# Windowed attention and a gated feed-forward on one core: products without a reader on TensorE, a shorter start on DVE and SP, and a weights' conversion with one operation written otherwise

## The chip, the cores and the metric

The kernel runs on one core of one Trainium2 chip. The time is device time in microseconds (us) of one execution; lower is better. The engines are TensorE (PE, with its weight loads as PEld), VectorE (DVE), ScalarE (ACT), GpSimd (POOL) and SyncE (SP), which here only issues transfers.

## The reference

Attention over 4 batches, 8 heads, 768 positions and 64 channels a head, with a window of 128 positions and 4 sink positions, then a feed-forward layer from 512 to 2048 and back to 512 over all 3072 positions. All inputs are float32, n_sink and window are 64-bit integers.

```python
scores = matmul(q, k.T) / sqrt(64)
keep = (pos_k < n_sink) | ((rel >= 0) & (rel < window))   # rel = pos_q - pos_k
a = softmax(where(keep, scores, -1e9))
x = matmul(a, v)                       # heads side by side: 3072 x 512
h = x @ w_in                           # 3072 x 2048
g = h * clip(h + 3, 0, 6) / 6
out = g @ w_out                        # 3072 x 512
```

## The kernel before

The attention is cut into 48 units: 4 batches, 3 blocks of 256 positions (u) and 4 pairs of heads (p). A unit's stages are named by letters: A loads K, Q and V from DRAM; B splits K and Q into a high and a low part; C makes the scores on TensorE (L292 or L297), adds the mask and takes the row's extreme on DVE (L299), the exponential on ACT (L321), sum and reciprocal on DVE (L323, L324) and the division (L307 on ACT, L309 on DVE); D turns the result on TensorE (L341) and copies it out (L35); E multiplies it with V (L399) and splits the result into xh and xl (L35, L415). The first eight units with u = 0 are "plain": they are kept in f32 and multiplied in f32, where the later ones work in fp32r on high and low parts.

After four units of a block its feed-forward follows: eight times 24 products with w_in (L437), the gate on ACT and DVE (L443, L444, L41, L446), and 24 products with w_out (L457). The steps of this part are drained between the stages of the attention by the order string in L530.

The weights arrive as 64-bit words (the float32 pairs of `load_part`, L143) and are converted on the chip, 32 pieces of 128x512 values: two passes on ACT (L150, magnitude; L154, count), two on DVE (L156 takes the sign into the upper half of the count's word, L158 joins the shifted magnitude with it), one on ACT for the high part (L35) and one on DVE for the low part (L161). A piece passes through the buffers `st` (3 of them) and `wt` (3). `WN` (L532) says how many pieces are asked for in each unit.

At the start POOL makes two ramps (`rel`, `col`) and the identity, ACT's queue loads n_sink and window (`raw`), DVE makes the masks out of them (L101 to L111), and POOL makes masks for the later units (m_t0, m_t1). DVE also makes a flag out of n_sink and window (L564 to L570) that chooses a general path at the end, which these inputs do not take. Each engine loads the flag into a register (L574).

The order on each engine is not the order of the code. A scheduler lists the instructions by what is ready and by the place in the code, and each engine then runs its list strictly in order, waiting at each entry for what it needs.

Of the kernel before, what the change touches and what calls it, by code (L numbers as in the profile page):

```python
# [9 lines left out]
F32 = mybir.dt.float32  # L10
F32R = mybir.dt.float32r
I32 = mybir.dt.int32
BF16 = mybir.dt.bfloat16
U16 = mybir.dt.uint16
U32 = mybir.dt.uint32
ALU = mybir.AluOpType
# [3 lines left out]
P = 128  # L20
SK = 16
WMAX = 128
SCALE = 0.125
BIG = 1.0e30


# [18 lines left out]
def attn_ffn_kernel(ctx: ExitStack, tc: tile.TileContext, qx, kx, vx, vfx, vsx, n_sink, window, w_in, w_out, out):  # L45
    nc = tc.nc
# [8 lines left out]
    const = ctx.enter_context(tc.tile_pool(name="const", bufs=1))  # L55
    fast = ExitStack()
    work = fast.enter_context(tc.tile_pool(name="work", bufs=2))
    ps = fast.enter_context(tc.tile_pool(name="ps", bufs=8, space=PSUM))
# [4 lines left out]
    relf = rel.rearrange("p a b -> p (a b)")  # L63
# [5 lines left out]
    ident_r = const.tile([P, P], F32R, name="ident_r")  # L69
    ident0 = work.tile([P, P], F32, tag="st", name="ident0", bufs=3)  # L70
    make_identity(nc, ident0)
# [3 lines left out]
    nc.vector.memset(three, 3.0)  # L75


    raw = const.tile([P, 2, 2], I32, name="raw")
    nc.scalar.dma_start(out=raw[:, 0, :], in_=n_sink.bitcast(I32).partition_broadcast(P))
    nc.scalar.dma_start(out=raw[:, 1, :], in_=window.bitcast(I32).partition_broadcast(P))  # L80
    rawf = const.tile([P, 2, 2], F32, name="rawf")
# [6 lines left out]
                                   op0=ALU.mult, op1=ALU.add)  # L88
# [3 lines left out]
    W2 = 2 * P + SK  # L92
    WP = 2 * P + 2 * SK
    m_t0 = work.tile([P, W2], BF16, name="m_t0", bufs=1)
    m_t1 = work.tile([P, W2], BF16, name="m_t1", bufs=1)
# [3 lines left out]
    own, prev, snk = relf[:, P:2 * P], relf[:, 2 * P:3 * P], colf[:, P:2 * P]  # L99
# [6 lines left out]
    def bias_from(dst, keep, engine=nc.vector):  # L106
        engine.tensor_scalar(out=dst, in0=keep, scalar1=-1.0, scalar2=BIG, op0=ALU.add, op1=ALU.mult)

# [4 lines left out]
    bias_from(m_01[:, P:2 * P], own)  # L113
    bias_from(m_t0[:, 0:P], prev, nc.gpsimd)
    bias_from(m_t0[:, P:2 * P], own, nc.gpsimd)
    bias_from(m_t0[:, 2 * P:W2], snk[:, 0:SK], nc.gpsimd)
    nc.gpsimd.tensor_copy(out=m_t1[:, 0:P], in_=m_t0[:, 0:P])
    nc.gpsimd.tensor_copy(out=m_t1[:, P:P + SK], in_=m_t0[:, 2 * P:W2])
    nc.gpsimd.tensor_copy(out=m_t1[:, P + SK:W2], in_=m_t0[:, P:2 * P])

# [11 lines left out]
    def load_part(hi, lo, src, rows, at):  # L132
# [4 lines left out]
        if not wide:  # L137
            st = like(work.tile([P, 512], F32, tag="st", name="st", bufs=3))
# [7 lines left out]
        ft = it.bitcast(F32)  # L146
        half = st.rearrange("p n w -> p (n w)").bitcast(U16).rearrange("p (n w) -> p n w", w=4)

# [6 lines left out]
                             bias=7.5 * 2.0 ** -18 - 0.5)  # L155
        nc.vector.tensor_scalar(out=half[:, :, 1], in0=half[:, :, 3], scalar1=0x8000, scalar2=None,  # L156
                                op0=ALU.bitwise_and)
        nc.vector.scalar_tensor_tensor(out=it, in0=it, scalar=3, in1=low,  # L158
# [17 lines left out]
    ssc = work.tile([P, 2, P], F32R, name="ssc", bufs=1)  # L176
    nc.gpsimd.memset(vs.bitcast(F32), 0.0)
    nc.gpsimd.memset(ssc.bitcast(F32), 0.0)

# [335 lines left out]
    def slot_C(s, h, t):  # L515
        if 0 <= s < NS:
            C_score(s, h, t)
            if t == 1:
                C_soft(s, h)

    def slot_E(s, h):
# [11 lines left out]

    for s in range(NS + 2):
        for step in ORDER.split():
            if step == "-":
# [25 lines left out]

    fl = const.tile([P, 4], F32, name="fl")
    nc.vector.tensor_scalar(out=fl[:, 0:1], in0=ns_f, scalar1=float(SK), scalar2=None, op0=ALU.is_gt)  # L564
# [164 lines left out]
```

## Time and profile before

| | us |
|---|---|
| three runs, median | 764.99 (764.61 to 767.12) |
| the profiled execution | 765.18 |
| its span, first to last instruction | 763.3 |
| PE busy | 728.7 (95%) |
| PEld busy | 648.1 (85%) |
| DVE busy | 505.8 (66%) |
| ACT busy | 458.1 (60%) |
| POOL busy | 4.0 (1%) |

The rows shown in the prediction are of five kinds. A row of the page names an engine and 40 slices of the span with their busy tenths. A row of the timeline has start and length in us, engine, line, operation, the tile written and the tiles read, the shape, and in brackets how long the engine was idle before it and what ended that. A row of the chain of waits has start, length and what the last-ending chain of work was doing. A row of groups has line, engine, operation, shape and count, then busy us and mean ns, then idle us before it. A row of stages has a stretch of the span and the busy time of each engine in it.

### The profile page before, as it was taken

Reading aid. Unit: us, or ns where it says so; the run is one execution under the profiler, and the core shown is the slowest. Engines: PE = TensorE matmul, PEld = TensorE weight load, DVE = VectorE, ACT = ScalarE, POOL = GpSimd, SP = SyncE. Lnnn points to the kernel's source line nnn. Section 1 sums busy time; section 2 is a strip of 40 time slices with the busy share of each in tenths; the row PEclk is TensorE's granted clock in tenths of the full one; section 3 lists DMA queues with packets and bytes.
Section 4 is the critical chain, followed back from the end, with each engine's and each line's share of the span. In section 5 each row is a group of like instructions: output and inputs, shape, how many; then the busy total and the mean of one; then the engine's idle time right before and its main releaser. Section 6 shows DMA issues by size and latency. Waiting matters only on the chain.

```text
span 763.3 us, 13907 instructions
## 1 busy us (share of the span) xinstructions
PE 728.7 (95%) x4832; PEld 648.1 (85%) x4832; DVE 505.8 (66%) x1434; ACT 458.1 (60%) x1115; POOL 4.0 (1%) x17
## 2 busy tenths in 40 slices
PE   4999888889999999999999999999999999999996
PEld 2677677679999999999889999899889989999895
DVE  4679999967677766765776776765676776542331
ACT  4788889776766755755666666755665665511211
POOL 2000000000000000000000000000000000000000
PEclk9999999999999999999999999999999999999998
DMA  5456878455454544532644545434554442000000
GB/s 187 121 165 217 238 212 237 138 142 132 128 134 122 134 125 105 140 95 67 166 110 114 143 107 127 120 82 102 146 130 116 128 114 72 15 15 1 28 1 32
DMA packets 57134, 89.87 MB, mean 118 GB/s; under 512 B 8672, under 2 KB 40416, under 8 KB 57056
## 3 DMA queue, kind: packets, MB, share of 16 engines
q1 hardware_dynamic: 56768, 88.90, 43.1%
q8 instruction: 40, 0.66, 0.4%
q14 instruction: 38, 0.31, 0.1%
q10 hardware_dynamic: 288, 0.00, 0.0%
HBM read 41.68 MB, written 6.29 MB: 63 GB/s over the span
## 4 chain that ended last, share of the span: by engine, by line
PE 78%; DVE 10%; ACT 5%; DMA 3%; issue 2%; SPq 1%; ACTq 0%; DVEq 0%
PE o L457 30%; PE hps L437 30%; PE av L399 7%; PE pt L341 4%; PE sp L297 4%; PE sp L292 2%; DMA K<-kt 1%; ACT Pt L307 1%; DVE st L156 1%; ACT Pt L321 1%; DVE wt L158 1%; DVE gf L444 1%; DVE Pt L299 1%; DMA raw<-in_window_dram 1%; DVE g L446 1%
## 5 line engine op out<-in xcount | busy, mean ns | idle before, releaser
L437 PE MATMUL hps<-xh,wih 128*128 128x256 f32 x768 | 219.9, 286 | 2.1 <-ACT wih L35 1.9
L437 PE MATMUL hps<-xh,wil 128*128 128x256 f32 x768 | 216.1, 282 | 1.6 <-DVE wil L161 1.6
L437 PE MATMUL hps<-xl,wih 128*128 128x256 f32 x768 | 215.5, 281 | 0.0
L457 PE MATMUL o<-woh,gh 128*128 128x512 f32 x384 | 156.2, 407 | 6.6 <-DVE gh L41 2.4
L457 PE MATMUL o<-woh,g 128*128 128x512 f32 x384 | 152.8, 399 | 1.9 <-DVE g L446 1.9
L457 PE MATMUL o<-wol,gh 128*128 128x512 f32 x384 | 152.5, 397 | 0.0
L437 PEld LDWEIGHTS hps<-xh,wih 128*128 128x128 f32 x768 | 145.7, 190 | 5.3 <-ACT wih L35 3.9
L437 PEld LDWEIGHTS hps<-xh,wil 128*128 128x128 f32 x768 | 145.2, 189 | 3.4 <-DVE wil L161 3.3
L437 PEld LDWEIGHTS hps<-xl,wih 128*128 128x128 f32 x768 | 145.6, 190 | 1.4
L321 ACT ACTIVATE Pt<-Pt,nb 128x272 f32<-128x272 f32 (+2 forms) x160 | 81.1, 507 | 73.3 <-DVE nb L299 71.3
L443 ACT ACTIVATE gf<-hps,three 128x512 f32<-128x512 f32 x96 | 65.9, 686 | 88.9 <-PE hps L437 88.4
L444 DVE SCALAR_TENSOR_TENSOR gf<-gf,hps 128x512 f32<-128x512 f32 x96 | 66.0, 687 | 67.0 <-ACT gf L443 65.8
L457 PEld LDWEIGHTS o<-woh,g 128*128 128x128 f32 x384 | 72.6, 189 | 21.8 <-DVE g L446 5.1
L457 PEld LDWEIGHTS o<-woh,gh 128*128 128x128 f32 x384 | 72.6, 189 | 19.1 <-DVE gh L41 3.1
L299 DVE CUSTOM_DVE_ANT_0 Pt<-sp,m_t 128x272 f32<-128x272 f32 x128 | 55.8, 439 | 49.5 <-PE sp L297 49.0
L307 ACT ACTIVATE Pt<-Pt,rc 128x272 f32<-128x272 f32 (+2 forms) x158 | 72.1, 502 | 25.9 <-DVE rc L324 24.7
L457 PEld LDWEIGHTS o<-wol,gh 128*128 128x128 f32 x384 | 72.6, 189 | 11.1 <-DVE wol L161 0.3
L446 DVE TENSOR_TENSOR g<-gf,gh 128x512 fp32r<-128x512 f32 x96 | 66.2, 690 | 1.1
L30 DVE TENSOR_TENSOR pl<-pt,ph 128x512 fp32r<-128x512 f32 (+1 forms) x80 | 52.8, 661 | 18.4 <-ACT ph L35 17.8
L297 PE MATMUL sp<-K,Q 128*128 128x272 f32 (+2 forms) x320 | 64.1, 288 | 0.7 <-DMA Q<-qt 0.4
L35 ACT ACTIVATE ph<-pt 128x512 fp32r<-128x512 f32 (+1 forms) x80 | 46.3, 578 | 29.5 <-PE pt L341 28.2
L297 PEld LDWEIGHTS sp<-K,Q 128*128 128x128 f32 x320 | 53.2, 189 | 8.1 <-DVE gf L444 0.7
(91 smaller groups left out, 944.0 us busy)
## 6 DMA issues: line engine op xcount, KB each, us to landing
K<-kt SPq DMA_DIRECT2D x128, 200.0 KB, 3.5
Q<-qt SPq DMA_DIRECT2D x160, 64.0 KB, 2.4
st<-in_w_in_dram SPq DMA_DIRECT2D x16, 512.0 KB, 4.7
st<-in_w_out_dram SPq DMA_DIRECT2D x16, 512.0 KB, 5.0
kr<-in_kx_dram SPq DMA_DIRECT2D x32, 200.0 KB, 2.6
qr<-in_qx_dram SPq DMA_DIRECT2D x48, 128.0 KB, 2.2
vr<-in_vx_dram SPq DMA_DIRECT2D x32, 192.0 KB, 2.6
out_dram<-ost SPq DMA_DIRECT2D x24, 256.0 KB, 2.3
```

The lines of the kernel that those rows point to most:

```text
L30: lo_engine.tensor_tensor(out=lo, in0=src, in1=hi.bitcast(F32), op=ALU.subtract)
L35: nc.scalar.mul(out=out, in_=src, mul=scale)
L297: nc.tensor.matmul(out=sp[:, 0:w], lhsT=Q[:, h, t * P:(t + 1) * P], rhs=K[:, h, part, k0c:k0c + w], start=(part == 0), stop=(part == 1))
L299: nc.vector.tensor_tensor_reduce(out=cell(s, h, t, 0, w), in0=sp[:, 0:w], in1=m[:, 0:w], scale=-SCALE, scalar=3.0e38, op0=ALU.add, op1=ALU ...
L307: nc.scalar.mul(out=blk, in_=blk, mul=c)
L321: nc.scalar.activation(out=blk, in_=blk, func=AF.Exp, scale=-1.0, bias=nb[:, i:i + 1], accum_out=sm[:, i:i + 1])
L399: nc.tensor.matmul(out=o, lhsT=l, rhs=r, start=(j == 0 and (h == 0 or not plain(s))), stop=(j == len(seq) - 1 and (h == 1 or not plain(s))))
L437: nc.tensor.matmul(out=hp[:, half, :], lhsT=l, rhs=r, start=(j == 0), stop=(j == n - 1))
L443: nc.scalar.activation(out=gf, in_=hp, func=AF.Relu, bias=three, scale=1.0)
L444: nc.vector.scalar_tensor_tensor(out=gf, in0=gf, scalar=6.0, in1=hp, op0=ALU.min, op1=ALU.mult)
L446: eng(GLO, state["n"] * NP).tensor_tensor(out=g, in0=gf, in1=gh.bitcast(F32), op=ALU.subtract)
L457: nc.tensor.matmul(out=acc, lhsT=l[:, f, ts_], rhs=r[i][:, f, :], start=(i == 0 and f == 0 and j == 0), stop=(i == NFP - 1 and f == 1 and ...
```

## The change

Two batches of ten products without a reader are put on TensorE (`keep_busy`): one ahead of the first scores, one behind the exponentials of the second head of unit 0. They multiply the ramp `rel` with itself in f32 and write a PSUM tile that nothing reads. The load of window goes from ACT's queue to SP's. The identity's scratch takes the buffer `kt` instead of one of the three `st`. The flag's scratch takes one of the three rotating buffers `nb`, so its operations can only follow the last units that use them. The later masks and two clearings are written into a function that is called at the head of unit 3. L156 and its 16-bit view give way to one operation on 32-bit words that masks the sign and joins it with the count.

```diff
+WARM = (10, 10)
...
-    ident0 = work.tile([P, P], F32, tag="st", name="ident0", bufs=3)
+    ident0 = work.tile([P, P], F32, tag="kt", name="ident0", bufs=1)
...
+    def keep_busy(n):
+
+        idle = ps.tile([P, 512], F32, tag="bank", name="idle")
+        for _ in range(n):
+            nc.tensor.matmul(out=idle[:, 0:P], lhsT=relf[:, 0:P], rhs=relf[:, 0:P], start=True, stop=True)
+
+    keep_busy(WARM[0])
...
-    nc.scalar.dma_start(out=raw[:, 1, :], in_=window.bitcast(I32).partition_broadcast(P))
+    nc.sync.dma_start(out=raw[:, 1, :], in_=window.bitcast(I32).partition_broadcast(P))
...
-    bias_from(m_t0[:, 0:P], prev, nc.gpsimd)
-    bias_from(m_t0[:, P:2 * P], own, nc.gpsimd)
-    bias_from(m_t0[:, 2 * P:W2], snk[:, 0:SK], nc.gpsimd)
-    nc.gpsimd.tensor_copy(out=m_t1[:, 0:P], in_=m_t0[:, 0:P])
-    nc.gpsimd.tensor_copy(out=m_t1[:, P:P + SK], in_=m_t0[:, 2 * P:W2])
-    nc.gpsimd.tensor_copy(out=m_t1[:, P + SK:W2], in_=m_t0[:, P:2 * P])
...
-        nc.vector.tensor_scalar(out=half[:, :, 1], in0=half[:, :, 3], scalar1=0x8000, scalar2=None,
-                                op0=ALU.bitwise_and)
+        nc.vector.scalar_tensor_tensor(out=low, in0=high, scalar=-2 ** 31, in1=low,
+                                       op0=ALU.bitwise_and, op1=ALU.bitwise_or)
...
-    nc.gpsimd.memset(vs.bitcast(F32), 0.0)
-    nc.gpsimd.memset(ssc.bitcast(F32), 0.0)
+
+    def later_constants():
+
+        bias_from(m_t0[:, 0:P], prev, nc.gpsimd)
...
+        nc.gpsimd.memset(vs.bitcast(F32), 0.0)
+        nc.gpsimd.memset(ssc.bitcast(F32), 0.0)
...
             if t == 1:
                 C_soft(s, h)
+                if s == 0 and h == 1:
+                    keep_busy(WARM[1])
...
     for s in range(NS + 2):
+        if s == 3:
+            later_constants()
...
-    fl = const.tile([P, 4], F32, name="fl")
+    fl = work.tile([P, 4], F32, tag="nb", name="fl", bufs=3)
```

The order on TensorE at the start of the program, before (sp are scores, pt the turned probabilities):

```order
L292 MATMUL sp<-kr,qr 128x128
L292 MATMUL sp<-kr,qr 128x256
L292 MATMUL sp<-kr,qr 128x128
L292 MATMUL sp<-kr,qr 128x256
L341 MATMUL pt<-ident_r,Ph 128x128 x4
```

and now (the line numbers of the changed kernel are up to 14 higher, so L302 is L292 and L351 is L341):

```order
L81 MATMUL idle<-rel 128x128 x10
L302 MATMUL sp<-kr,qr 128x128
L302 MATMUL sp<-kr,qr 128x256
L302 MATMUL sp<-kr,qr 128x128
L302 MATMUL sp<-kr,qr 128x256
L81 MATMUL idle<-rel 128x128 x10
L351 MATMUL pt<-ident_r,Ph 128x128 x4
```

The two batches stand ahead of the first scores and between them and the first transpositions; nothing else moves there.

The order on ACT at the start, before (Ph is the f32 score tile, st and wt are buffers of the weights' conversion):

```order
L79 DMA raw<-in_n_sink_dram 128x2
L80 DMA raw<-in_window_dram 128x2
L321 ACT_TABLE_LOAD
L321 ACTIVATE Ph,sm<-Ph,nb 128x128
L321 ACTIVATE Ph,sm<-Ph,nb 128x256
L321 ACTIVATE Ph,sm<-Ph,nb 128x128
L321 ACTIVATE Ph,sm<-Ph,nb 128x256
L307 ACTIVATE Ph<-Ph,rc 128x256
L150 ACTIVATE wt<-st 128x512
```

and now (L151 is L150, L155 is L154, L331 is L321):

```order
L87 DMA raw<-in_n_sink_dram 128x2
L151 ACT_TABLE_LOAD
L151 ACTIVATE wt<-st 128x512
L155 ACTIVATE st<-st 128x512
L151 ACTIVATE wt<-st 128x512
L155 ACTIVATE st<-st 128x512
L151 ACTIVATE wt<-st 128x512
L35 ACTIVATE wih_111<-wt 128x512
L155 ACTIVATE st<-st 128x512
L331 ACTIVATE Ph,sm<-Ph,nb 128x128
L331 ACTIVATE Ph,sm<-Ph,nb 128x256
```

Seven operations of the weights' conversion now stand ahead of the first exponential.

The order on DVE behind the first two heads' score tiles, before:

```order
L299 ISA Ph,nb<-sp,m_90 128x256
L299 ISA nb 128x1
L323 TENSOR_SCALAR sm<-sm 128x2
L324 RECIPROCAL rc<-sm 128x2
L309 TENSOR_SCALAR Ph<-Ph,rc 128x128
```

and now (L309 is L299, L162 is L161, L159 is L158, L157 stands in the place of L156, L333, L334 and L319 are L323, L324 and L309):

```order
L309 ISA Ph,nb<-sp,m_101 128x256
L309 ISA nb 128x1
L162 TENSOR_TENSOR wil_119<-wt,wih_111 128x512
L333 TENSOR_SCALAR sm<-sm 128x2
L159 SCALAR_TENSOR_TENSOR wt<-wt,st 128x512
L334 RECIPROCAL rc<-sm 128x2
L333 TENSOR_SCALAR sm<-sm 128x2
L157 SCALAR_TENSOR_TENSOR st<-st 128x512
L319 TENSOR_SCALAR Ph<-Ph,rc 128x128
```

Three operations of the weights' conversion now stand between the last score tile and the first division.

More of the change, by code (lines that the diff above doesn't have):

```diff
@@ L13 @@
 BF16 = mybir.dt.bfloat16
-U16 = mybir.dt.uint16
 U32 = mybir.dt.uint32
@@ L146, in load_part @@
         ft = it.bitcast(F32)
-        half = st.rearrange("p n w -> p (n w)").bitcast(U16).rearrange("p (n w) -> p n w", w=4)
         nc.scalar.activation(out=ft, in_=high.bitcast(F32), func=AF.Abs, scale=2.0 ** -112)
@@ L176, in attn_ffn_kernel @@
     ssc = work.tile([P, 2, P], F32R, name="ssc", bufs=1)
-    nc.gpsimd.memset(vs.bitcast(F32), 0.0)
-    nc.gpsimd.memset(ssc.bitcast(F32), 0.0)
+    def later_constants():
+        bias_from(m_t0[:, 0:P], prev, nc.gpsimd)
+        bias_from(m_t0[:, P:2 * P], own, nc.gpsimd)
+        bias_from(m_t0[:, 2 * P:W2], snk[:, 0:SK], nc.gpsimd)
+        nc.gpsimd.tensor_copy(out=m_t1[:, 0:P], in_=m_t0[:, 0:P])
+        nc.gpsimd.tensor_copy(out=m_t1[:, P:P + SK], in_=m_t0[:, 2 * P:W2])
+        nc.gpsimd.tensor_copy(out=m_t1[:, P + SK:W2], in_=m_t0[:, P:2 * P])
+        nc.gpsimd.memset(vs.bitcast(F32), 0.0)
+        nc.gpsimd.memset(ssc.bitcast(F32), 0.0)
     def batch_loads(b):
```

## The prediction

> **What bounds the kernel now.** I read the clock row of the page first, then TensorE's rows in order of time, then the chain of waits, then busy time by stage. The page's clock row says full speed from the first slice on:
>
> ```profile
> PEclk9999999999999999999999999999999999999998
> ```
>
> TensorE's own rows say otherwise. In the first block of the feed-forward part (L437) equal 128x256 products start 0.22 us apart, and a microsecond later 0.12 us apart:
>
> ```profile
> 48.19 0.41 PE L437 MATMUL hps<-xh,wil 128*128 128x256 f32 x1
> 48.41 0.41 PE L437 MATMUL hps<-xh,wih 128*128 128x256 f32 x1
> ...
> 49.57 0.28 PE L437 MATMUL hps<-xh,wih 128*128 128x256 f32 x1
> 49.69 0.28 PE L437 MATMUL hps<-xl,wih 128*128 128x256 f32 x1
> ```
>
> So until 49.3 us TensorE works at half its later pace, and the row does not show it. The chain of waits says the same: one set of f32 scores (L292) or of f32 products with V (L399) takes 1.58 us there, and 0.85 us later on.
>
> ```profile
> 22.69 1.58 PE sp L292 x4
> ...
> 26.17 1.58 PE sp L292 x4
> 27.74 1.58 PE av L399 x4
> ```
>
> ```profile
> 59.68 0.85 PE sp L292 x4
> 60.53 0.85 PE av L399 x4
> ```
>
> By stage (columns: length, then busy us and instructions of PE, PEld, DVE, ACT, POOL, then granted clock, DMA share, GB/s):
>
> ```profile
> 12.00:50.00 38.00, 36.04 (x107) 24.38 (x108) 23.17 (x82) 28.53 (x74) 0.00 (x0) 1.00 0.49 156
> ...
> 80.00:100.00 20.00, 15.31 (x84) 12.56 (x83) 18.32 (x49) 17.16 (x43) 0.00 (x0) 0.91 0.85 244
> ...
> 120.00:140.00 20.00, 17.69 (x114) 14.66 (x112) 18.94 (x44) 17.44 (x39) 0.00 (x0) 1.00 0.76 238
> 140.00:180.00 40.00, 35.70 (x240) 31.59 (x241) 30.16 (x84) 26.15 (x65) 0.00 (x0) 0.96 0.46 124
> 180.00:300.00 120.00, 119.81 (x860) 110.76 (x859) 85.05 (x246) 79.13 (x194) 0.00 (x0) 1.00 0.50 127
> ```
>
> Three stages: from 12 to 50 us a slow TensorE (95% busy), then to about 150 us DVE with ACT close behind (the weights' conversion: 92 to 95%), then TensorE at full pace. The last stage does the same work in both kernels, so what the change wins or loses before 160 us comes out one for one at the end.
>
> **The change part by part.** *Start of ACT.* In the kernel before, the weights' loads stand on SP behind the branch flag, and ACT takes its first exponentials first (the start of the row is in us, then how long it took):
>
> ```profile
> 6.86 0.15 DVE L564 TENSOR_SCALAR fl<-nw 128x1 f32<-128x1 f32 x1
> ...
> 7.56 0.28 DVE L101 TENSOR_SCALAR rel<-rel,nw 128x128 f32<-128x128 f32 x1
> ...
> 9.15 0.80 SPq L143 DMA_DIRECT2D st<-in_w_in_dram  x2
> ...
> 9.50 0.28 DVE L299 CUSTOM_DVE_ANT_0 Ph<-sp,m 128x128 f32<-128x128 f32 x1
> ...
> 9.82 0.40 ACT L321 ACTIVATE Ph<-Ph,nb 128x128 f32<-128x128 f32 x1 [6.86 <-DVE nb L299]
> ...
> 11.98 1.36 PE L341 MATMUL pt<-ident_r,Ph 128*128 128x128 f32 x4 [4.60 <-DVE Ph L309]
> ...
> 12.97 0.66 ACT L150 ACTIVATE wt<-st 128x512 f32<-128x512 f32 x1 [0.58 <-DMA st<-in_w_in_dram]
> ```
>
> Taking the flag's six operations away brings the masks forward by 7.56 - 6.86 = 0.70 us, and that is worth nothing by itself: in the new order of ACT the first exponential stands behind seven operations of the conversion, three L150, three L154 and one L35, which need the weights.
>
> ```profile
> L154 ACT ACTIVATE st<-st 128x512 int32<-128x512 uint32 x32 | 21.3, 665 | 0.0
> L150 ACT ACTIVATE wt<-st 128x512 f32<-128x512 f32 x32 | 21.3, 665 | 2.4 <-DMA st<-in_w_out_dram 1.8 <-DMA st<-in_w_in_dram 0.6
> ...
> L35 ACT ACTIVATE wih<-wt 128x512 fp32r<-128x512 f32 x16 | 10.0, 625 | 2.2 <-DVE wt L158 2.1
> ```
>
> They take 3 x 0.665 + 3 x 0.665 + 0.625 = 4.6 us. The first weights landed 12.97 - 9.15 = 3.8 us after their issue. They now go out behind seven issues of 0.4 us and a little (0.80 for the two in the row above), at about 4 us, but also behind 1 MB of K, Q and V; I take 8.5 us for the landing (bounds: 4 + 3.8 = 7.8, and 9.8 if the transfers before them delay them by 2 us). The first exponential then starts at 8.5 + 4.6 = 13.1 us instead of 9.82: 3.3 us later. Behind the exponentials DVE now does one L161, one L158 and one operation in the place of L156 ahead of the first L309, which the first transposition waits for:
>
> ```profile
> L156 DVE TENSOR_SCALAR st<-st 128x512 uint16<-128x512 uint16 x32 | 24.0, 750 | 3.4 <-ACT st L154 3.1
> L158 DVE SCALAR_TENSOR_TENSOR wt<-wt,st 128x512 int32<-128x512 int32 x32 | 22.0, 689 | 0.5
> ...
> L161 DVE TENSOR_TENSOR wil<-wt,wih 128x512 fp32r<-128x512 f32 x16 | 11.0, 687 | 1.1 <-ACT wih L35 1.1
> ```
>
> That is about 2.1 us, of which I take 1.0 to lie under the exponentials: 1.1 us more. The first transposition so moves from 11.98 to about 16.4 us: **+4.4 us** (bounds +3.7 and +5.7), and the slow TensorE behind it, 95% busy, carries this to 50 us.
>
> *What is bought with it.* The first and the fifth L444 frame the stage in which DVE bounds the kernel:
>
> ```profile
> 51.60 0.69 DVE L444 SCALAR_TENSOR_TENSOR gf<-gf,hps 128x512 f32<-128x512 f32 x1 [0.39 <-ACT gf L443]
> ...
> 81.65 0.68 DVE L444 SCALAR_TENSOR_TENSOR gf<-gf,hps 128x512 f32<-128x512 f32 x1
> ```
>
> By the first DVE has done, counting its rows in order, 10 sign steps, 9 L158 and 8 L161 instead of 7, 7 and 6: 3 x 0.75 + 2 x 0.69 + 2 x 0.69 = 5.0 us of DVE's work ahead of it that stood behind it. By the fifth the counts are level again (19, 18, 18 against 19, 19, 19). Between the two DVE bounds the kernel, so the lead is worth **-5.0 us** there (bounds: 0 if something else bounds that stage, -6.4 if all three conversions are whole).
>
> *Sign and count joined.* 32 L156 of 0.75 us become 32 operations like L158, on three strided operands instead of two. Where the next operation needs the result, DVE went on after 0.78 us, where it does not, after 0.53 us:
>
> ```profile
> 76.51 0.74 DVE L156 TENSOR_SCALAR st<-st 128x512 uint16<-128x512 uint16 x1
> 77.04 0.45 DVE L299 CUSTOM_DVE_ANT_0 Ph<-sp,m 128x256 f32<-128x256 f32 x1
> ...
> 85.69 0.75 DVE L156 TENSOR_SCALAR st<-st 128x512 uint16<-128x512 uint16 x1 [0.22 <-ACT st L154]
> 86.47 0.69 DVE L158 SCALAR_TENSOR_TENSOR wt<-wt,st 128x512 int32<-128x512 int32 x1
> ```
>
> With 0.69 us the joined one saves 0.06 in the first case and may lose some 0.07 in the second. With some 24 of the first and 8 of the second: 1.4 - 0.5 = **-0.9 us** (bounds -1.9, all of the first kind, and +1.0, if the third strided operand costs 0.06 more).
>
> *Products without a reader.* Each is a 128x128 product in f32, two instructions. From the 1.58 us of four instructions over 768 columns, one of 128 takes about 0.26 to 0.29 us at the slow pace, so ten take 5.2 to 5.8 us. The first ten need only the IOTA of L65, which ends at 0.84 + 0.24 = 1.1 us, and end at about 6.9. The first scores could begin at 5.72 before:
>
> ```profile
> 0.84 0.24 POOL L65 IOTA rel<- 128x128 f32 x1 [0.39 <-POOLq L712]
> ...
> 5.72 1.66 PE L292 MATMUL sp<-kr,qr 64*128 64x128 f32 x8 [5.72 <-DMA qr<-in_qx_dram]
> ```
>
> The 1.2 us are covered: the scores end by 8.6 us, DVE reaches them after 9 us. Were that cover gone, they would cost 1.2 us. The second ten end at about 14.4 us, before the first transposition at 16.4; with a first exponential at 9.82, as now, they would have cost 2.4 us. **0**, unless they change TensorE's pace. I say they do not, for long enough: from 22.69 to 29.32 us TensorE does f32 products without a pause, 6.6 us, more than half of them on all 128 rows, and stays slow; the fp32r products of one block of L437 brought the faster pace (first rows above). And a pace gained is lost in idle time:
>
> ```profile
> 80.32 0.81 PE L399 MATMUL av<-pf,VF 128*128 128x256 f32 x4
> 83.28 0.53 PE L457 MATMUL o<-woh,gh 128*128 128x512 f32 x1 [2.14 <-DVE sm L323]
> ```
>
> After these 2.14 idle us the granted clock falls (0.91 over that stage, above), and the changed kernel idles 2 us or more ahead of its first transposition.
>
> The Trainium skill (TensorE: Matmul & The Clock Gate, Part 1, the HAM clock gate) puts it as time: "Whatever you issue in your first ~3.4 µs runs at 1.2 GHz; everything after runs at 2.4 GHz." By that the first batch alone would bring the fast pace. The trace agrees for fp32r, and disagrees for the f32 stretch of 6.6 us.
>
> *The rest.* The identity in another buffer frees the third weights' buffer at once (in the loads above). The window's load ahead of K on SP puts the scores some 0.45 us later, covered by the masks. The later masks and the two clearings stand on POOL in the same order as before; POOL works 4.0 us in all, so that edit is 0. The flag's operations now stand late on DVE, before the last stage, and SP reads the flag with six output transfers behind it: 1.0 us of DVE under a TensorE that is 99.8% busy: 0.
>
> **Sum.** +4.4 - 5.0 - 0.9 = -1.5 us. The profiled execution took 765.18 us (span 763.3 and 1.9 around it) and lies 0.2 us above the median of 764.99. 765.18 - 1.5 - 0.2 = **763.5 us**; its own range, with the bounds above, is 760 to 767.
>
> **Rivals.** *TensorE gets fast early and stays so.* This is the skill's rule worked out here. For it: the batches run on full 128 rows for some 13 us, a stretch that the trace before does not have (its scores use 64 rows). Against it: the 6.6 us, and that the f32 stretches alone would have to hold the pace. The head would then be bound by ACT: 28.53 us busy in 12 to 50 us, plus 2.5 conversions of about 1.95 us more: 33 us from 16.4, so the first L444 at about 50 instead of 51.6. That is -1.5, with the lead and the sign -1.5 - 5.0 - 0.9 = -7.4: 757.6 us.
>
> *The delay stays and the lead is lost.* In the middle stage DVE also waits for transfers:
>
> ```profile
> 132.95 6.03 DMA K<-kt
> 139.03 3.96 DMA vr<-in_vx_dram
> ```
>
> If earlier weights only move the waits of SP's queue (K, Q and V stand in it behind the weights' loads, which wait for a free buffer), the 5.0 us of DVE's work turn into idle time at this place. Against it: DVE is 92 to 95% busy there, so there is little idle time to turn them into. 4.4 - 0.9 = +3.5: 768.5 us. It decides from the point where these 10 us end no earlier than now.
>
> *The change does not do what it says:* the conversions, though first in order, do not come earlier because their loads land late; then the delay is small too, and only the sign counts: 764.1 us.
>
> **Chances.** Forecast 0.45, early fast TensorE 0.33, lost lead 0.17, only the sign 0.05. A measurement of this kernel tells 0.3%, 2.3 us, from no change: below 762.7 is faster, above 767.3 slower. Of the forecast's 0.45 some 0.18 lie below 762.7, 0.02 above 767.3. Faster 0.33 + 0.18 = 0.51; slower 0.17 + 0.02 and a rest of 0.01 = 0.20; same 0.29. The range runs from 756.5, which holds most of the second case, to 767.5, which leaves out most of the third.
>
> **What would show it.** In the changed profile: a first exponential near 13 us and a first transposition near 16.4 (late loads: later still); scores and products with V of 1.58 us up to the first L437, against 0.85 if the batches work; the first L444 near 56 us, and the fifth, at 81.65 before, at about 80.5 (74 with a fast TensorE, 85 with a lost lead); the joined operation near 0.69 us. The forecast is wrong if the pace changes before 45 us, or if ACT does not wait for weights at the start.

## The result, and the profile after

The changed kernel takes **776.73 us** (median of 4, 774.42 to 777.48) against 765.43 us (median of 4, 764.61 to 767.12) of the kernel before, run beside it: a ratio of 1.0138, 95% interval 1.0117 to 1.0159. It is slower by some 11 us, outside the predicted range. Its profiled execution took 774.42 us, 9.2 us more than that of before, and is the fastest of the four; the traces below account for these 9.2 us.

The head of the changed kernel, TensorE in order of time (these lines stand ten lines lower in the changed kernel: L302 is L292, L351 is L341, L409 is L399, L447 is L437, L467 is L457, L454 is L444; L81 are the products without a reader):

```profile
1.13 4.21 PE L81 MATMUL idle<-rel 128*128 128x128 f32 x20 [1.13 <-POOL rel L65]
5.76 0.93 PE L302 MATMUL sp<-kr,qr 64*128 64x128 f32 x8 [0.42 <-DMA qr<-in_qx_dram]
6.62 2.50 PE L81 MATMUL idle<-rel 128*128 128x128 f32 x20
16.60 1.24 PE L351 MATMUL pt<-ident_r,Ph 128*128 128x128 f32 x4 [7.48 <-DVE rc L334]
...
20.26 1.65 PE L409 MATMUL av<-pf,VF 128*128 128x256 f32 x4
```

The products do bring the fast pace: the eight instructions of the first scores take 0.93 us instead of 1.66. Then TensorE idles 7.48 us for the first transposition and the pace is gone: the products with V take 1.65 us for four, as before. The clock row of the page shows the half pace now, in its first three slices of 19.3 us, which it did not in the kernel before:

```profile
PEclk7569989999999999999999999999999999999999
```

ACT behind that idle time (its first conversion, L151, and behind the seven operations of the conversion its first exponential, L331):

```profile
9.43 0.66 ACT L151 ACTIVATE wt<-st 128x512 f32<-128x512 f32 x1 [6.96 <-DMA st<-in_w_in_dram]
...
13.61 0.40 ACT L331 ACTIVATE Ph<-Ph,nb 128x128 f32<-128x128 f32 x1
```

The joined sign operation takes what was predicted (mean 688 ns):

```profile
L157 DVE SCALAR_TENSOR_TENSOR st<-st 128x512 int32<-128x512 int32 x32 | 21.9, 688 | 3.6 <-ACT st L155 3.5
```

The stages behind the head, cut at the same gates (the first L444, the one at 81.65 us, which is the fourth in the trace and not the fifth as the prediction counts, and the one at 145.43 us). Before (length, busy us of PE, PEld, DVE, ACT, POOL, granted clock, DMA share, GB/s):

```profile
51.60:81.65 30.05, 29.28 (x168) 23.06 (x166) 28.17 (x77) 27.14 (x64) 0.00 (x0) 1.00 0.65 195
81.65:145.43 63.78, 55.55 (x346) 46.63 (x347) 59.53 (x143) 54.37 (x121) 0.00 (x0) 0.97 0.78 227
```

After:

```profile
57.10:82.84 25.74, 25.17 (x143) 19.75 (x142) 22.50 (x60) 21.58 (x53) 0.00 (x0) 1.00 0.59 188
82.84:152.76 69.92, 60.09 (x358) 50.81 (x358) 61.29 (x153) 55.65 (x126) 0.00 (x0) 0.93 0.70 207
```

The first of the two stages is 4.3 us shorter: the lead of the conversions is real, and the changed kernel is only 1.2 us behind at 82.84 us. The second is 6.1 us longer. DVE's idle time in it is 8.6 us (69.92 - 61.29) against 4.3 us before; the other 1.8 us are DVE's own work, 61.29 us against 59.53. TensorE idles 9.8 us against 8.2, and its granted clock is 0.93 against 0.97: as an estimate from these two figures, 4.9 us of full speed are missing (0.07 x 69.92) instead of 1.9 (0.03 x 63.78). The largest single place, TensorE first:

```profile
99.46 0.73 PE L467 MATMUL o<-woh,gh 128*128 128x512 f32 x2 [1.79 <-ACT woh L35]
...
101.52 0.63 PE L467 MATMUL o<-woh,g 128*128 128x512 f32 x1
...
105.81 0.39 PE L467 MATMUL o<-woh,g 128*128 128x512 f32 x1
110.86 0.58 PE L447 MATMUL hps<-xh,wih 128*128 128x256 f32 x1 [4.66 <-ACT wih L35]
```

and ACT at the same time:

```profile
102.69 0.52 ACT L317 ACTIVATE Pt<-Pt,rc 128x272 f32<-128x272 f32 x1 [1.99 <-DVE rc L334]
...
106.01 0.69 ACT L453 ACTIVATE gf<-hps,three 128x512 f32<-128x512 f32 x1 [2.37 <-PE hps L447]
...
106.90 0.66 ACT L151 ACTIVATE wt<-st 128x512 f32<-128x512 f32 x1
...
110.17 0.63 ACT L35 ACTIVATE wih<-wt 128x512 fp32r<-128x512 f32 x1 [0.93 <-DVE wt L159]
```

TensorE idles 1.79 us, its next products take 0.63 us instead of 0.39, ACT stands 2.37 us ahead of a gate that these products make late, the next conversion (L151) is queued behind that gate, and TensorE then idles 4.66 us for this very conversion. Before, the largest wait of TensorE in this stage was 2.14 us. A second place follows at 122.72 us, where TensorE waits for the sink positions' V (`raw_s`, split into `vs`); before, no wait for it in this stage reaches 0.2 us. Behind it the products of L467 are slow again (0.63 us):

```profile
122.72 0.39 PE L409 MATMUL av<-pz,vs 128*128 128x256 f32 x1 [1.91 <-DVE vs L30]
...
125.00 0.63 PE L467 MATMUL o<-woh,g 128*128 128x512 f32 x1
```

From about 180 us on the two kernels run nearly in parallel, but not quite: 7.1 us apart at 315 us, 9.2 at the last outputs.

### The profile page after: what moved, and what is told of

It reads as the page before. It is cut to its first block, busy times and chain, and to the rows that moved or that the text cites. A ratio compares the mean times of both kernels' runs of the same rounds, so it can differ in the third digit from the quotient of the medians.

```text
span 772.7 us, 13996 instructions
## 1 busy us (share of the span) xinstructions
PE 737.9 (96%) x4872; PEld 659.7 (85%) x4872; DVE 505.5 (65%) x1434; ACT 456.8 (59%) x1115; POOL 3.9 (1%) x17
## 4 chain that ended last, share of the span: by engine, by line
PE 76%; DVE 7%; ACT 7%; DMA 5%; issue 2%; SPq 1%; ACTq 0%; DVEq 0%
PE o L467 30%; PE hps L447 29%; PE av L409 6%; PE sp L307 4%; PE pt L351 4%; DMA st<-in_w_in_dram 2%; PE sp L302 2%; ACT Pt L317 1%; ACT Pt L331 1%; DMA st<-in_w_out_dram 1%; ACT wt L151 1%; DVE wt L159 1%; DMA raw_s<-in_vsx_dram 1%; DMA Q<-qt 1%; DVE gf L454 1%
## 5 line engine op out<-in xcount | busy, mean ns | idle before, releaser
L447 PE MATMUL hps<-xh,wih 128*128 128x256 f32 x768 | 222.0, 289 | 6.1 <-ACT wih L35 5.7
L447 PE MATMUL hps<-xh,wil 128*128 128x256 f32 x768 | 217.5, 283 | 0.0
L447 PE MATMUL hps<-xl,wih 128*128 128x256 f32 x768 | 216.6, 282 | 0.0
L467 PE MATMUL o<-woh,gh 128*128 128x512 f32 x384 | 156.7, 408 | 5.6 <-DVE gh L41 3.8
L447 PEld LDWEIGHTS hps<-xh,wih 128*128 128x128 f32 x768 | 145.4, 189 | 10.2 <-ACT wih L35 7.9
L467 PE MATMUL o<-woh,g 128*128 128x512 f32 x384 | 153.6, 401 | 0.4 <-DVE g L456 0.4
L467 PE MATMUL o<-wol,gh 128*128 128x512 f32 x384 | 152.9, 399 | 0.0
L447 PEld LDWEIGHTS hps<-xl,wih 128*128 128x128 f32 x768 | 145.5, 189 | 1.3
L447 PEld LDWEIGHTS hps<-xh,wil 128*128 128x128 f32 x768 | 145.0, 189 | 0.9 <-DVE wil L162 0.5
L331 ACT ACTIVATE Pt<-Pt,nb 128x272 f32<-128x272 f32 (+2 forms) x160 | 81.2, 507 | 77.5 <-DVE nb L309 75.9
L453 ACT ACTIVATE gf<-hps,three 128x512 f32<-128x512 f32 x96 | 66.0, 687 | 91.6 <-PE hps L447 90.9
L454 DVE SCALAR_TENSOR_TENSOR gf<-gf,hps 128x512 f32<-128x512 f32 x96 | 65.9, 687 | 72.1 <-ACT gf L453 70.7
L467 PEld LDWEIGHTS o<-woh,g 128*128 128x128 f32 x384 | 73.3, 191 | 19.1 <-DVE g L456 2.2
L309 DVE CUSTOM_DVE_ANT_0 Pt<-sp,m_t 128x272 f32<-128x272 f32 x128 | 55.7, 439 | 51.1 <-PE sp L307 50.2
L467 PEld LDWEIGHTS o<-woh,gh 128*128 128x128 f32 x384 | 73.1, 190 | 17.8 <-DVE gh L41 4.5
L467 PEld LDWEIGHTS o<-wol,gh 128*128 128x128 f32 x384 | 73.5, 192 | 10.9
```

The costliest lines, as they stand in the source:

```text
L309: nc.vector.tensor_tensor_reduce(out=cell(s, h, t, 0, w), in0=sp[:, 0:w], in1=m[:, 0:w], scale=-SCALE, scalar=3.0e38, op0=ALU.add, op1=ALU ...
L331: nc.scalar.activation(out=blk, in_=blk, func=AF.Exp, scale=-1.0, bias=nb[:, i:i + 1], accum_out=sm[:, i:i + 1])
L447: nc.tensor.matmul(out=hp[:, half, :], lhsT=l, rhs=r, start=(j == 0), stop=(j == n - 1))
L453: nc.scalar.activation(out=gf, in_=hp, func=AF.Relu, bias=three, scale=1.0)
L454: nc.vector.scalar_tensor_tensor(out=gf, in0=gf, scalar=6.0, in1=hp, op0=ALU.min, op1=ALU.mult)
L467: nc.tensor.matmul(out=acc, lhsT=l[:, f, ts_], rhs=r[i][:, f, :], start=(i == 0 and f == 0 and j == 0), stop=(i == NFP - 1 and f == 1 and ...
```

## Experiments: order, or work

**One edit taken out.** Each edit changes the order in which the scheduler lays out the engines' instructions, so four kernels leave out one edit each (the late masks and the late flag were not left out singly).

```
no_products:     keep_busy(...) removed
no_joined_sign:  the 16-bit TENSOR_SCALAR of before in the place of the joined operation
no_ident_buffer: ident0 = work.tile(..., tag="st", bufs=3) again
no_window_move:  nc.scalar.dma_start(out=raw[:, 1, :], ...) again
```

> The changed kernel without the twenty products that nobody reads; everything else of the change stays. By the theory of the order (nothing that was added costs; the loss comes from the instruction streams, which each edit reshuffles): in this kernel's order one conversion operation instead of seven stands ahead of ACT's first exponential, and SP issues raw_s's load (L183 before) among the K loads, as before the change, so the first exponential is near 10.5 us, nothing is lost between 82 and 142 us, and the time is 763 to 766 us. By the theory of the products' own cost (work or clock): also about 766. By the theory that the joined sign operation costs, or that the identity's buffer does (weights start too early): the loss stays, about 775 us.

> The changed kernel with the old 16-bit sign operation. Order: seven conversion operations still stand ahead of the first exponential, but raw_s's load stands among the K loads again. By the theory of the order with SP's place of raw_s as the main loss: the head's 5 us stay lost, the lead gives back some 4, the 7 us between 82 and 142 us are not lost: 766 to 768 us. By the theory of the products, or of the identity's buffer: about 775 us. By the theory that the joined operation itself costs: 766 us as well, so this run tells the sign from the products and the buffer, and only with the next two from the order.

> The changed kernel with the identity back in the weights' third buffer. Order: one conversion operation ahead of the first exponential, but raw_s's load stands ahead of all four K loads, behind more weights' loads, as in the changed kernel. By the theory of the order with SP's place of raw_s as the main loss: first exponential near 10.5 us, but 5 to 8 us lost between 82 and 142 us: 769 to 773 us. By the theory that the early third weights' load is the cause: 764 to 766 us. By the theory of the products or of the sign: about 775 us.

> The changed kernel with the window's load back on ACT's queue. Order: eight conversion operations ahead of the first exponential, raw_s's load among the K loads as before the change. By the theory of the order with SP's place of raw_s as the main loss: head as in the changed kernel, no loss between 82 and 142 us: 766 to 768 us. By the theories that products, sign or the identity's buffer cost by themselves: about 775 us.

Measured, against 765.53 us of before: no_products 768.33 us (ratio 1.0043, 1.0027 to 1.0058), no_joined_sign 769.11 (1.0045, 1.0023 to 1.0067), no_ident_buffer 775.26 (1.0119, 1.0093 to 1.0144), no_window_move 769.63 (1.0051, 1.0035 to 1.0067). Three different edits, each taken out, give most of the loss back, so no single edit's work carries it. The kernels split as the place of raw_s's load on SP's queue does, as expected, though each is 1 to 3 us slower than the theory said, and no_ident_buffer came out at the 775 us of the rival of products or sign, which the first two kernels rule out. That place is not the cause of no_ident_buffer's loss: it is 5.6 us late at the L444 of 81.65 us already (87.23), and issues raw_s at 120.6 us. What the place is worth in the changed kernel, where TensorE waits 1.91 us for it, stays open: no run moved this load alone.

**Order and work apart.** Two kernels were tied to each other's order: at the end of the program each instruction gets an edge to the one ahead of it on its engine in the other kernel's order (the code is shortened here). The edges fix the issue order and add no wait.

```
+    for j, k in zip(at, at[1:]):          # at: the other kernel's order of this engine
+        tc.add_manual_dep(mine[k], mine[j].name, DependencyInfo(NoSync, DATA), reason="order")
```

> All edits of the change (products, joined sign, the identity's and the window's place, late flag and late masks), but every instruction that both kernels have is tied, engine by engine, to its neighbour of the kernel before (edges that set the issue order alone, without a wait), so that all five engines issue in the order of the kernel before; the products stand where the changed kernel has them, ahead of and behind the first scores. By the theory of the order: 762 to 766 us, no different from before (the joined sign alone is good for -0.9), first exponential near 9.8 us, first transposition near 12. By the theory that the added work or the buffers cost by themselves: 772 to 776 us.

> None of the edits' work: the operations of the kernel before, without products, with the old sign operation, the identity in the weights' buffer and the window on ACT's queue, but tied, engine by engine, to the order of the changed kernel. By the theory of the order: 772 to 777 us, with the first exponential behind seven conversion operations (13 to 14 us) and the same idle stretch of TensorE near 106 us. By the theory that the work costs: 764 to 767 us.

Measured, against 765.85 us: all edits in the old order 767.38 us (1.0018, 1.0005 to 1.0031), 1.4 us above the range expected; no edit in the new order 771.27 us (1.0065, 1.0044 to 1.0085), a little less than expected. The new order without any edit makes the changed kernel's picture, the late first transposition and the same idle stretch (TensorE; L431 is L341, L527 is L437):

```profile
17.07 1.24 PE L431 MATMUL pt<-ident_r,Ph 128*128 128x128 f32 x4 [9.94 <-DVE rc L414]
...
112.98 0.58 PE L527 MATMUL hps<-xh,wih 128*128 128x256 f32 x1 [4.95 <-ACT wih L125]
```

The same points of the program in five profiled executions (us; the last column is a later experiment):

| point | before | after | no edit, new order | all edits, old order | old order, old places |
|---|---|---|---|---|---|
| first transposition | 11.98 | 16.60 | 17.07 | 10.29 | 10.94 |
| first L444 | 51.60 | 57.10 | 58.56 | 50.78 | 51.74 |
| L444 at 81.65 | 81.65 | 82.84 | 83.92 | 81.22 | 82.40 |
| L444 at 145.43 | 145.43 | 152.76 | 153.51 | 144.89 | 145.50 |
| eighth output | 315.15 | 322.26 | 322.04 | 314.88 | 314.99 |
| last two outputs | 756.00 | 765.18 | 763.03 | 758.10 | 756.25 |

The order costs 7.0 us (756.00 to 763.03), all of it before 180 us. The edits' work costs nothing up to 315 us (0.3 us are gained), and 2.1 us (758.10) grow evenly behind that. Together 9.1 of the 9.2 us. That this sum closes is partly luck: the changed kernel's trace is its fastest execution and that of the new order lies 1 us above its median. The medians give 5.4 and 1.5 us of the 11.3; the other 4.4 were not settled.

**One place of the order.** Is the idle stretch at 110 us one misplaced instruction? The changed kernel's own order, with one weights' load moved ahead of eight copies of K and Q on SP, and then with the conversion that uses it moved as well:

```
SP:   ... kr qr [st] K K K K Q Q Q Q  st st ...       (one_load_moved)
ACT:  woh [L151 L155] L317 kt [wih] gf qt ...         (one_conversion_earlier, with the load)
DVE:  ssc [L157 L159] kt gf qt gh g ...
```

> The changed kernel with its own order on all engines, but for one instruction: on SP the weights' load that it issues at 101.5 us, behind eight copies of K and Q (which wait for TensorE until 96 us), goes ahead of them, to about 93 us, as the kernel before has one at 91.36. By the theory that this place on SP's queue makes the largest loss (TensorE idle 4.66 us at 110.9 us for weights converted late, and half pace for some 3 us behind it): the idle time shrinks below 1.5 us and the time falls by 3 to 6 us against the changed kernel, to 769 to 772 us. By the rival, that the loss is spread over many waits and DVE's work bounds the stage anyway: less than 1 us, 774 to 776 us.

> The kernel with the one load moved on SP, and now the conversion that uses it as well: ACT's first two operations on that load go ahead of ACT's wait for rc (at 100.7 us, instead of behind gf, which waited for TensorE until 106), its rounding ahead of that gf, and DVE's two operations on it ahead of DVE's wait for the same gf; nothing else is moved. By the theory that an engine's own order holds the conversion back (data there, but the instruction queued behind one that waits for TensorE, while TensorE then waits for the conversion): the 4.66 us of idle TensorE near 106 to 111 us fall below 1.5 us, the half pace behind it goes, and the time is 770 to 773 us against 776.7. By the rival that DVE's and ACT's total work bounds the stage: the idle time only moves to the next place, 774 to 777 us.

The first took 776.66 us (1.0127, 1.0086 to 1.0168), so this theory fell. The load went out early enough, and the idle time stayed (SP's, ACT's and TensorE's rows; L543, L241, L537 are L453, L151, L447 of the changed kernel):

```profile
93.48 0.40 SPq L235 DMA_DIRECT2D st<-in_w_in_dram  x1
...
107.33 0.69 ACT L543 ACTIVATE gf<-hps,three 128x512 f32<-128x512 f32 x1 [2.60 <-PE hps L537]
...
108.22 0.66 ACT L241 ACTIVATE wt<-st 128x512 f32<-128x512 f32 x1
...
112.18 0.39 PE L537 MATMUL hps<-xh,wih 128*128 128x256 f32 x1 [4.66 <-ACT wih L125]
```

The data is there; the conversion is queued behind ACT's wait. With the conversion moved too the time is 775.35 us (1.013, 1.0109 to 1.0151), as the rival said. The stretch of 4.66 us shrank, and others took its place:

```profile
92.57 0.39 PE L537 MATMUL hps<-xh,wih 128*128 128x256 f32 x1 [2.34 <-ACT wih L125]
...
109.37 0.39 PE L537 MATMUL hps<-xh,wih 128*128 128x256 f32 x1 [0.93 <-ACT wih L125]
113.27 0.52 PE L537 MATMUL hps<-xh,wil 128*128 128x256 f32 x1 [3.28 <-DVE wil L252]
```

So the 6 us do not hang on this one load or this one conversion. With the run of no edit in the new order they belong to the order of the stage, in which ACT, DVE and TensorE wait for each other in turn. Which feature of that order is worth most was not found.

## Experiments: the drift behind 315 us

In all kernels with the edits one product of L437 is a little longer. The row of `hps<-xl,wih` from 320 to 750 us, before:

```profile
L437 PE MATMUL hps<-xl,wih 128*128 128x256 f32 x501 | 140.0, 279 | 0.0
```

From the starts of some 1,800 such products that follow each other between 180 and 750 us: 118.8 ns apart before and with no edit in the new order, 120.4 after, 120.5 with all edits in the old order. (The expectations below put the two at 119.4 and 121.0 ns; the figures in the text are the ones that these traces give.) There are 2,304 of them, so 1.6 ns each make 3.7 us, some two thirds of it behind 315 us. The flag's edit moves the whole pool of work tiles down by 32 bytes, and the identity's edit reshuffles the tiles in it, so the places in memory were suspected. flag_alone is the kernel before with the flag's edit; all_edits_aligned undoes it in the kernel with all edits in the old order:

```
-    fl = const.tile([P, 4], F32, name="fl")
+    fl = work.tile([P, 4], F32, tag="nb", name="fl", bufs=3)      (and back, in all_edits_aligned)
```

> The kernel before with nothing but the flag's edit: its operations late, and its 4 numbers in a buffer of the attention's pool instead of the constants' pool. The issue order of TensorE and ACT stays as before, and every tile of that pool stands 32 bytes lower in the memory than before (the moving operands xh and xl of L437 on 32 instead of 0 modulo 64). By the theory that the place in memory costs (the products of L437 start 121.0 us apart per thousand in all kernels with the late flag, 119.4 in the two without): 767 to 768.5 us, with the loss growing evenly from unit to unit, and 121 ns. By the rival that the drift comes from products, sign or window: 764.5 to 766, 119.4 ns.

> The kernel with all edits in the order of the kernel before, but for the flag's four numbers, which go back into the constants' pool (the flag's operations stay late), so that xh and xl stand on 0 modulo 64 bytes again. By the theory of the place in memory: the drift of 2.1 us goes, 764 to 766 us, L437 at 119.4 ns. By the rival that the late flag operations themselves or another edit cause the drift: 767 to 768 us, as without this step.

flag_alone took 766.42 us against 765.01 (1.0009, 0.9995 to 1.0022): not told from zero by time, but its products start 121.0 ns apart and its last outputs are 2.3 us late in the trace, 0.8 of them from the head (first L444 at 52.44 us).

```profile
L437 PE MATMUL hps<-xl,wih 128*128 128x256 f32 x497 | 140.4, 282 | 0.0
```

all_edits_aligned took 767.59 us (1.0037, 1.0024 to 1.0051), 119.8 ns: no gain, although xh and xl stand on 0 modulo 64 again. (Its flag operations were not tied and stand at 6 us as before, so it undoes the flag's edit in full, not its place alone as its expectation says.) A multiple of 64 bytes is thus not the rule. The products of L457 moved too: of those that start less than 250 ns apart between 180 and 750 us, the mean distance is 232.9 ns before, 232.2 after, 229.8 in flag_alone and 233.5 in all_edits_aligned. There are 1,152 of them, so flag_alone gains some 3.6 us at L457 of the 5.1 that it loses at L437, which fits a time that hardly shows the drift. The last step puts the identity back too, so that the tiles stand where they stood before:

> Products, joined sign, the window's load on SP and the later masks, in the order of the kernel before, and with the tiles of the kernel before at their old addresses: the identity is back in the weights' buffer and the flag's four numbers in the constants' pool. By the theory that the places in memory make the drift: L437 back at 119.4 ns, no loss behind 320 us, 764 to 765 us. By the rival that the products, the sign or the order of code make it: 767 us and 120.5 to 121 ns, as in the two kernels with the old order so far.

765.77 us against 766.02 (ratio 1.0000, 0.9990 to 1.0011), 118.7 ns, and of the 2.1 us of drift 0.3 are left at the last outputs (the table's last column):

```profile
L537 PE MATMUL hps<-xl,wih 128*128 128x256 f32 x501 | 139.9, 279 | 0.0
```

So the drift comes from where the tiles lie, and the products, the joined sign, the window's load and the later masks together are worth nothing that can be measured, in the old order (in this kernel too the flag's operations stand at 6 us). What it is about the addresses stays open.

## Experiments: TensorE's pace in the head

The first rows of the changed kernel contradicted the prediction on the pace. Does it hang on the rows of the array? The twenty products with 64 rows (one execution, in the old order):

```
-  lhsT=relf[:, 0:P], rhs=relf[:, 0:P]
+  lhsT=relf[0:64, 0:P], rhs=relf[0:64, 0:P]
```

> All edits in the old order, but the twenty products without a reader use 64 rows of the array instead of 128 (same columns, same count). By the theory that the number of rows in work brings the pace: the first scores take 1.6 us for eight instructions instead of 0.93, and the ten products before them take 5.2 us or more instead of 4.1. By the rival that any uninterrupted work of 4 us does: 0.93 us and 4.1 us as with 128 rows.

768.82 us, and the pace does not come:

```profile
5.80 1.66 PE L392 MATMUL sp<-kr,qr 64*128 64x128 f32 x8
7.21 4.47 PE L171 MATMUL idle<-rel 64*128 64x128 f32 x20
```

Rows it is, as far as one execution shows: 1.66 and 4.47 us against 0.93 and 2.50. (The ten products ahead took 4.63 us, less than the 5.2 expected; with 128 rows they took 4.09 to 4.64 us, so their own time does not tell the two apart. The first scores alone would not either: behind ten products on 128 rows they took 1.54 us in no_window_move. The second batch does: 2.5 us there too.) Next the pace was held on purpose, all in the old order, with WARM = (10, 21, 6): 21 products behind the first scores and 6 behind each of the first eight sets of products with V.

```
+            if s < 4:
+                keep_busy(WARM[2])         # behind E_av(s, h)
```

> All edits in the order of the kernel before, with more products that nobody reads: 21 instead of 10 behind the first scores (to fill the time to the first transposition), and 6 behind each of the first eight sets of products with V. By the theory that f32 products on 128 rows bring the fast pace and only idle time or the 64-row scores lose it: scores and products with V take 0.85 us instead of 1.58 through the head, and the first L444 of the kernel before (51.6 us) comes 2 to 5 us earlier; the time is 757 to 764 us, since DVE and ACT then bound the head. By the rival, that the f32 mix of the head drops the pace even so: the 59 further products of about 0.5 us each at the slow pace cost 15 to 25 us in the head, and the time is 775 to 790 us.

764.63 us against 765.85 (0.9980, 0.9964 to 0.9996). Behind an idle stretch of 1.50 us the pace is lost for some 2 us (the products at 16.06 us and the scores at 18.76); from 19.8 us on the scores take 0.92 us throughout the head. But the 6 products stand 1.5 us in the way each time, and the first L444 comes at 49.37 us:

```profile
16.06 2.77 PE L171 MATMUL idle<-rel 128*128 128x128 f32 x12
18.76 1.14 PE L392 MATMUL sp<-kr,qr 64*128 64x128 f32 x4
...
26.94 0.92 PE L392 MATMUL sp<-kr,qr 64*128 64x128 f32 x4
27.79 0.92 PE L499 MATMUL av<-pf,VF 128*128 128x256 f32 x4
28.55 1.50 PE L171 MATMUL idle<-rel 128*128 128x128 f32 x12
```

> The kernel with the steady products, with 32 bytes more among the constants ahead of the weights: that puts xh and xl, and the weights too, on 0 modulo 64 bytes (the weights stood on 32 in both kernels, and L457 reads woh and wol as its moving operand). By the theory of the place in memory for L437 alone: the drift of 2.1 us goes, 762 to 763 us. If L457 gains as L437 does (from 236 to 239 ns per product to 2 or 3 ns less, over some 2300 products): 757 to 761 us. By the rival (the place in memory does nothing): 764 to 766 us as without it.

This one (`three = const.tile([P, 16], ...)[:, 0:1]`) took 763.11 us against 765.01 (0.9975, 0.9963 to 0.9987), products of L437 120.4 ns apart: its gain lies in the head of that execution (first L444 at 46.88 us; the pace does not lapse there), and neither L437 nor L457 gained by the multiple of 64. That the time lies close to the 762 to 763 us of the first theory is luck. Then 3 products instead of 6, with the old places:

> The kernel above with steady products, 21 behind the first scores and 3 (instead of 6) behind each of the first eight sets of products with V, at the old addresses. By the theory that idle stretches of about 1.5 us and more lose the pace, and that the products stand in the way themselves (1.5 us for six, eight times): the pace holds, the head gets shorter by 3 to 6 us against the kernel with six, the first L444 of the kernel before comes at 43 to 46 us, and the time is 757 to 761 us. By the rival that the 64-row scores lose the pace unless enough products stand between them: it is lost before 30 us, scores at 1.58 us again, first L444 at 49 to 52 us and 763 to 767 us.

**758.31 us** against 766.02 (0.9898, 0.9878 to 0.9918): 1% faster than the kernel before. (Of the step from six products some 2 us are the places, by the drift above.) Its profiled execution, the slowest of five (762.42), lost the pace for a while:

```profile
14.41 0.44 PE L441 MATMUL pt<-ident_r,Ph 128*128 128x128 f32 x2 [1.93 <-ACT Ph L407]
...
20.36 1.65 PE L499 MATMUL av<-pf,VF 128*128 128x256 f32 x4
...
27.97 0.92 PE L499 MATMUL av<-pf,VF 128*128 128x256 f32 x4
```

Eight further products in just that idle stretch, behind the first score of the second pair:

```
+            if (s, h, t) == (1, 0, 0):
+                keep_busy(8)
```

> The kernel with few steady products (21 behind the first scores, 3 behind each set of products with V, old order, old places) with eight further products in the stretch of 1.93 idle us behind the first scores of the second pair. By the theory that an idle stretch of about 2 us loses the pace while the head's mixed work does not: the pace holds from the first products to the end of the head, no scores at 1.58 us, first L444 of the kernel before at 42.5 to 45 us, 755 to 758 us, with less spread than the 756.45 to 762.42 of the kernel without the eight. By the rival that the 64-row scores and the few products lose it: scores at 1.58 us between 15 and 24 us again and 758 to 762 us.

758.80 us against 765.27 (0.9931, 0.9904 to 0.9958), 755.68 to 762.35. In the profiled execution (755.68) the pace holds through the head, the first L444 comes at 44.09 us, 7.5 us earlier than before, and the last outputs 9.8 us earlier:

```profile
12.47 2.05 PE L171 MATMUL idle<-rel 128*128 128x128 f32 x16
14.48 0.44 PE L441 MATMUL pt<-ident_r,Ph 128*128 128x128 f32 x2
...
15.47 0.92 PE L499 MATMUL av<-pf,VF 128*128 128x256 f32 x4
```

But the median is no better than without the eight products, and the spread did not get smaller: the executions with 762.3 us have a mean granted clock of 0.986, the fastest 0.997. By that, and by the profiled execution without the eight (0.985, pace lost in the head), whether the pace survives the head seems to change from execution to execution; the slow ones here have no trace, and the eight products did not settle it.

## Why the prediction was wrong, point by point

- **The start of ACT: right.** First exponential 13.61 us (13.1 predicted; the weights landed 0.9 us later than taken, the seven operations took 0.4 us less), first transposition 16.60 (16.4), so +4.6 us (+4.4); the first L444 was 5.5 us late.
- **The lead: right in size as far as 82 us, wrong behind it.** Between the first L444 and the one at 81.65 it brought 4.3 us (5.0 predicted). The step that failed is the premise that DVE's work bounds the kernel to about 150 us: with the counts level at that gate, the -5.0 us were taken as kept and the stage behind it as unchanged. That stage took 69.92 us instead of 63.78. DVE's 92 to 95% were not a bound by its work: in the two stages together it had 3.9 us less to do (83.8 against 87.7 us) and idled 5.7 us more (11.9 against 6.1), with the engines waiting for each other. The prediction looked at the new order in the head and only counted operations behind it. Behind 180 us "one for one" held but for the drift (7.1 us at 315, 9.2 at the end).
- **Lost lead as a rival** named this (768.5 us, chance 0.17): DVE's work taken ahead turns into idle time. But it put it at K's and V's loads and took away the lead alone, and the idle time grew by more than the lead. The order costs 7.0 us at the end of the trace, not 3.5 or 4.4. Of the queue that it suspected one weights' load was moved, which changed nothing; raw_s's load on the same queue was not.
- **The joined sign: right for the operation** (0.69 us). The 0.9 us saved show in no total: at 104 us the kernels with all edits in the old order are 0.6 us ahead of before with one placing of the tiles and 0.6 behind with the old one.
- **The products: 0, for a wrong reason.** f32 products bring the pace if they use all 128 rows; that they changed nothing behind it is owed to the idle time, which lost the pace again (7.48 us), as the second half of the argument said. Ten of them took 4.2 us, not 5.2 to 5.8. The Trainium skill (TensorE: Matmul & The Clock Gate, Part 1, the HAM clock gate) has the pace come after about 3.4 us of work; the trace agrees for the products on 128 rows (the starts of their instructions go from 213 to 112 ns apart 3.6 us behind the first) and not for those on 64 (213 ns throughout).
- **Fast TensorE as a rival** (757.6 us, 0.33): its condition did not come about in the changed kernel. Where it was made to hold (gap_filled, in the old order, so without the late start and without the lead), the profiled execution gained 9.8 us and the median 6.5. From the first transposition to the first L444 it took 32.6 us (11.53 to 44.09), against 39.6 before and the 33 that the rival worked out with the lead's conversions in it.
- **The rest at 0: wrong by some 2 us.** Moving the flag's numbers and the identity was costed by their waits alone; the addresses that came of it put 1.6 ns on every product of L437.

## What to carry to other kernels

An edit to a program that a scheduler lays out is two edits, its work and a new order of everything behind it; tie the old order to the new work, and the new order to the old work, before you credit either (here the order made 7.0 us of the trace and 5.4 of the median; the work made nothing once the tiles stood at their old places). A stage in which two engines are 92% busy is not yet a bound: see whether the waits inside it run in a ring (TensorE on ACT's conversion, ACT on TensorE's gate), for then a lead at its start need not come out at its end. And if a stage runs at half pace, try few products on all rows between its steps rather than one batch at its start: 21 behind the first scores and three behind each of eight sets gained 1% here, the two batches of ten at the start nothing.

## What the runs showed of the hardware that was not expected

- f32 products on 128 rows bring the fast pace within 3 to 6 us of work, products on 64 rows do not (0.93 against 1.66 us for the first scores), and the kernel before worked from 12 to 46 us on a mix of the two and of transpositions without it.
- The pace was lost after 1.79 us of idle TensorE (0.63 us instead of 0.39 at 101.52 us) and after 1.93 us in the head. The Trainium skill (TensorE: Matmul & The Clock Gate, Part 1) gives about 3.4 us of idle time for that; the measurement decides: less is enough here. It is no fixed length, though: the same stretch of the program, 1.82 us in the kernel before and 1.81 in gap_filled, lost the pace in the first (equal products 0.41 us long behind it) and not in the second (0.28):

```profile
160.44 0.50 PE L457 MATMUL o<-woh,gh 128*128 128x512 f32 x1 [1.82 <-DVE gh L41]
...
164.20 0.41 PE L437 MATMUL hps<-xl,wih 128*128 128x256 f32 x1
```

```profile
152.55 0.50 PE L557 MATMUL o<-woh,gh 128*128 128x512 f32 x1 [1.81 <-DVE gh L131]
...
155.36 0.28 PE L537 MATMUL hps<-xl,wih 128*128 128x256 f32 x1
```

- The clock row read full for a head that ran at half pace, in the kernel before and with 64 rows; it fell below full in the head only where the fast pace had been reached and lost.
- Moving tiles by 32 bytes, or into another sequence, changes the distance between equal fp32r products from 118.8 to 119.8 to 121.0 ns (0.8 to 1.9%), and a start on a multiple of 64 bytes is not what decides it.
